# A dependence from a port-sharing VectorE operation to the GpSimd operation planned behind it, in both planned lists of a fused attention and MoE kernel

## The chip, the cores and the metric

The kernel runs on one core of a Trainium2 chip. A core has five instruction queues that run side by side: the profile calls them PE (TensorE, matrix multiplication), DVE (VectorE), ACT (ScalarE), POOL (GpSimd) and SP (SyncE, which here only starts DMA transfers). Each queue runs its instructions in order and waits on semaphores where it needs another queue's result. The metric is the device time of one execution in microseconds. The kernel before took 730.56 us (median of 3 runs, 727.94 to 731.85).

## The reference, cut to what matters

```python
def _attn_ref(x, state):                    # x (8, 8, 512, 64), state (8, 8, 32, 64)
    scale = 1.0 / np.sqrt(D)
    scores = scale * np.matmul(x, state.transpose(0, 1, 3, 2))
    ...                                     # softmax over the 32 states
    xread = np.matmul(a, state)
    scores2 = scale * np.matmul(state, x.transpose(0, 1, 3, 2))
    ...                                     # softmax over the 512 tokens
    sread = np.matmul(a2, x)
    return np.concatenate([xread, sread], axis=2)

def _moe_ref(x, w_in, w_out):               # x (4352, 512), w_in (512, 2048), w_out (2048, 512)
    h = x @ w_in
    g = h * np.cos(h)
    return g @ w_out
```

The attention output, with its heads laid side by side, is the x of the second part. Everything is float32.

## The kernel before, in words

The kernel walks over the 8 batches, two at a time (a pair), and at the end over the 256 rows of read states. For a batch it computes both softmaxes from the same scores, never forms xread, but multiplies the states with w_in first and the attention weights with that product. So a tile of h (128 of the 2048 columns, 512 tokens) is one or two PE products of `aT_all` (attention weights) with `sw_all` (states times w_in). ACT and DVE make g = h cos(h) of it, in the four steps `gate`, `gate2`, `gate3`, `gate4` (a rounding, a difference, a sine table, a product), and g lands in a quarter of `g_all`. From the second pair on the products with both weight matrices use a seven-product scheme instead of eight. The scheme needs sums and differences of its operands, and these sums are the work of POOL: `Product.sums` (halves of g, tile `g_all`), `sw_sums` (tiles `sw_all` and `swS_all`, needed by the next h tile) and `Product.total` (tile `held`, an output sum). Some sums are on DVE: `outer_sum` (tile `g_all`, 128x1024) and `halves` (tile `aS_all`).

The softmax of the next batch runs in the shadow of the tiles. Its places that matter here are: `spread1` (L357) writes a broadcast sum into the first half of the tile `xT`; `norm1` (L425) multiplies the attention weights by it on DVE (`aT_all<-aT_all,xT`, 128x1024, two inputs in SBUF); `turn_kept` (L438) then copies the turned second softmax on ACT into the same half of `xT`, so that this copy has to wait for norm1; and `reads` (L445) multiplies with the copy on PE (`at<-x_b,xT`).

The order on every queue is decided when the program is built, by two list planners with a cost for each operation. The first pair of batches is a list of tasks: `first_pair` (L1598) takes the tasks by due time and calls each one, which issues its instructions (the profile puts them all at L44, the line of the helper `Lane`). Everything after it is recorded on a tape, cut into works by `works_of` (L1776), ordered by `in_order` (L1823) and issued in the order of the planned starts (L1868 to L1870; the profile puts these at L1870). Both planners hold that POOL and certain DVE operations share a port of SBUF and don't run at once: in the first list those whose task is added with `shares`, in the second `tensor_tensor` and `scalar_tensor_tensor` works with no operand in PSUM (L1807). `lock` is the planned end of the last operation that used the port, and a sharing operation is planned no earlier (L1651, L1848, L1857). The plan fixes only the order within each queue. Between queues the built program waits for data alone.

POOL issues no DMA after the first four state loads. SP issues all the others in order, among them the weight blocks that PE reads (`g_all<-blocks_kept`) and the x loads into `xT`.

Of the kernel before, what the change touches and what calls it, by code (L numbers as in the profile page):

```python
# [22 lines left out]
def kernel(  # L23
# [8 lines left out]
    tape, taping, burst, exps_bursts = [], [False], [0], set()  # L32
    hbm_names = [a.name for a in (x, state, moe_w_in, moe_w_out, out)]

    class Lane:
        def __init__(self, name, engine):
            self.name, self.engine = name, engine

        def __getattr__(self, op):
            f = getattr(self.engine, op)  # L40

            def call(*args, **kw):
                if not taping[0]:
                    return f(*args, **kw)  # L44
                tape.append((self.name, op, f, args, kw, burst[0]))
            return call

    class Lanes:
        tensor, vector = Lane("pe", tc.nc.tensor), Lane("dve", tc.nc.vector)
# [941 lines left out]
    def warm(n, to):  # L991

        for _ in range(n):
            nc.tensor.matmul(out=to, lhsT=zeros[:, 0:P], rhs=zeros, start=True,
                             stop=True)
# [95 lines left out]
    dve, pool = nc.vector, nc.gpsimd  # L1091
    for n in range(B // 2):
        end = n == B // 2 - 1
# [468 lines left out]
    def link(tasks):  # L1562
        wrote, read = {}, defaultdict(list)
        for t in tasks:
            before = set()
            for r in t.reads:
                before.add(wrote.get(r))
            for w in t.writes:
                before.add(wrote.get(w))
                before.update(read[w])  # L1570
            before.discard(None)
            before.discard(t)
            t.before = list(before)
            for r in t.reads:
                read[r].append(t)
            for w in t.writes:
                wrote[w] = t
                read[w] = []
        after = defaultdict(list)
        for t in tasks:  # L1580
            for u in t.before:
                after[u].append(t)
        for t in reversed(tasks):
            t.due = 22.0 + PACE * t.due if t.due is not None else 1e9
            for u in after[t]:
                t.due = min(t.due, u.due - t.cost - 0.05)
        return after
# [10 lines left out]
    def first_pair():  # L1598
        nonlocal n_stages
        now[0] = FIRST - 1  # L1600
        tasks = first_pair_tasks()
        after = link(tasks)
        free = {"pe": START_PE, "act": 10.2, "dve": 12.8, "pool": 6.0,
                "sp": 23.0}
        arrived = {}
        for i, at_ in enumerate(ARRIVED):
            for r in ("".join(names_raw(i))).split():
                arrived[r] = at_
        waiting = {t: len(t.before) for t in tasks}
        ready = {t: 0.0 for t in tasks}  # L1610
        for t in tasks:
            for r in t.reads:
                if r in arrived:
                    ready[t] = max(ready[t], arrived[r])
            for w in t.writes:
                arrived.pop(w, None)
        can = [t for t in tasks if not waiting[t]]
        lanes = 22.0
        lock = 0.0
        cold = True  # L1620
        log = []
        while can:
            best = None
            for e in free:
                mine = [t for t in can if t.engine == e]
                if not mine:
                    continue
                starts = {}
                for t in mine:
                    asked = max(free[e], ready[t])  # L1630
                    shares = t.shares or e == "pool"
                    starts[t] = max(asked, lock) if shares else asked
                soon = min(starts.values())
                t = min((t for t in mine if starts[t] <= soon + NEAR),
                        key=lambda t: t.due + 8.0 * (starts[t] - soon))
                asked = max(free[e], ready[t])
                if best is None or (starts[t], asked) < best[0:2]:
                    best = starts[t], asked, t
            at_, _, t = best
            if t.engine == "pe":  # L1640
                idle = int((at_ - free["pe"] - .4) / .86)
                if t.writes[0] == "acc":
                    cold = False
                if cold and idle > 0:
                    warm(idle, acc[0])
            t.what()
            can.remove(t)
            end = at_ + t.cost
            free[t.engine] = end
            log.append((at_, t))  # L1650
            if t.shares or t.engine == "pool":  # L1651
                lock = end
            if t.engine == "sp":
                size = {"x": .13, "Q": 1.05, "B": .26, "r": .26}.get(
                    t.writes[0][0], .3)
                lanes = max(lanes, at_ + 1.3) + size / .36
                end = lanes - 1.8
            t.end = end
            for u in after[t]:
                waiting[u] -= 1  # L1660
                ready[u] = max(ready[u], end + lag(t, u))
                if not waiting[u]:
                    can.append(u)
        assert len(log) == len(tasks)
        n_stages = 5
        for at_ in [stage_at, sums_at, outer_at]:
            for step in [step for step in at_ if step < FIRST]:
                del at_[step]
        return log

    def names_raw(i):
        h = i % 2
        n = (2 * h, 2 * h + 1) if i < 4 else range(QT)
        return " ".join(f"Q{SLOTS[i]}_{k}" for k in n)
# [101 lines left out]
    def works_of(tape):  # L1776
        works, last, at_ = [], {}, 0.0
        wrote, read = {}, defaultdict(list)
        for engine, op, f, args, kw, n in tape:
            aps = [a for a in list(args) + list(kw.values())  # L1780
                   if isinstance(a, AP)]
            outs = [kw["out"] if "out" in kw else args[0]]
            if "accum_out" in kw:
                outs.append(kw["accum_out"])
            ins = [a for a in aps if not any(a is o for o in outs)]
            if op == "matmul" and not kw["start"]:
                ins.append(outs[0])
            exp = engine == "act" and kw.get("func") == ACTF.Exp
            w = last.get(engine)
            if not (w is not None and w.burst == n  # L1790
                    and (engine == "act" and n in exps_bursts
                         or engine == "pe" and works[-1] is w)):
                w = last[engine] = Work(engine, n, at_)
                works.append(w)
                if exp:
                    w.cost += 2.5
                if op == "matmul" and kw["lhsT"].partition_size() == D:
                    w.cost += .3
            w.calls.append((f, args, kw))
            w.cost += cost_of(engine, op, kw, aps)  # L1800
            if engine == "pe":
                at_ += cost_of(engine, op, kw, aps)
            if op == "dma_start":
                w.landing = landing(kw)
            if engine == "dve" and op in ("tensor_tensor",
                                          "scalar_tensor_tensor"):
                w.shares = all(a.space != PSUM for a in aps)  # L1807
            for cell in [c for a in ins for c in cells(a)]:
                if cell in wrote:
                    w.before.add(wrote[cell])  # L1810
                read[cell].append(w)
            for cell in [c for o in outs for c in cells(o)]:
                if cell in wrote:
                    w.before.add(wrote[cell])
                w.before.update(read[cell])
                wrote[cell] = w
                read[cell] = []
            w.before.discard(w)
        return works
# [3 lines left out]
    def in_order(tape, free):  # L1823
# [15 lines left out]
        while can:  # L1839
            best = None  # L1840
            for e in free:
# [4 lines left out]
                for w in mine:  # L1846
# [3 lines left out]
                w = min((w for w in mine if starts[w] <= soon + NEAR_LATER),  # L1850
                        key=lambda w: w.due + LATE * (starts[w] - soon))
                if best is None or starts[w] < best.start:
                    best, best.start = w, starts[w]
            w = best
            can.remove(w)
            end = free[w.engine] = w.start + w.cost
# [3 lines left out]
            for u in after[w]:  # L1860
# [4 lines left out]
                if not waiting[u]:  # L1865
                    can.append(u)
        assert len(log) == len(works)
        for w in sorted(log, key=lambda w: w.start):  # L1868
            for f, args, kw in w.calls:
                f(*args, **kw)  # L1870

    first_log = first_pair()
    singles.__exit__(None, None, None)
# [72 lines left out]
```

## Time and profile before

| | |
|---|---|
| device time, 3 runs | 727.94, 730.56, 731.85 us |
| device time of the profiled execution | 726.99 us |
| its span, first to last instruction | 725.2 us |
| PE busy | 701.0 us, 97% of the span |
| DVE, ACT, POOL busy | 508.9 (70%), 348.0 (48%), 540.2 (74%) us |
| mean granted TensorE clock | 0.992 |

A profile row of a group names the line, the engine, the operation, the tile it writes and the tiles it reads, the shape, how many there are, and after the bar the busy time and the mean duration of one. In a timeline the row begins with the start and the duration in us from the start of the span. In the view of waits a row says which engine waited for which producer, how long in total, how often, and the longest. In the view by stretches there follow, after the stretch and its length, the busy times of PE, PEld (weight loads), DVE, ACT and POOL with the number of instructions, then the granted TensorE clock as a share of the full one, the busy share of the DMA engines and their rate. What the duration of one DVE or POOL instruction shows includes time in which the port kept it out.

### The profile page before, as it was taken

How to read it: one execution, taken by the hardware profiler on the slowest of the kernel's cores; microseconds unless marked ns; L12 is line 12 of the kernel's file. 1: busy time of each engine (PE TensorE's matmuls, PEld its weight loads, DVE VectorE, ACT ScalarE, POOL GpSimd, SP SyncE). 2: the span in 40 equal slices, each digit the busy share in tenths (PEclk: the TensorE clock that was granted, in tenths of full speed). 3: DMA queues.
4: the chain of work that ended last, by engine and by line, in shares of the span. 5: the costliest groups of instructions: out<-in, count | busy, mean ns of one | idle time of the engine just before them, and what ended most of it. 6: DMA issues, size and time to landing. Idle time of an engine off the chain costs nothing.

```text
span 725.2 us, 10728 instructions
## 1 busy us (share of the span) xinstructions
PE 701.0 (97%) x3628; PEld 524.1 (72%) x3628; DVE 508.9 (70%) x698; ACT 348.0 (48%) x591; POOL 540.2 (74%) x524
## 2 busy tenths in 40 slices
PE   8898899999979999999999999999999999999997
PEld 4444344477857878787788787878788888888886
DVE  4899879987876687776986567878766476625630
ACT  5689876754543447444634554445634443211100
POOL 1466799578984998898998856998988848896500
PEclk9999999999989999999999999999999999999999
DMA  9966699756436754783258435762366345465851
GB/s 298 294 194 201 190 260 294 190 137 142 142 82 134 205 130 123 149 193 89 78 128 186 118 88 126 153 147 85 114 153 157 89 111 128 110 200 170 224 103 29
DMA packets 204022, 111.34 MB, mean 154 GB/s; under 512 B 149888, under 2 KB 166784, under 8 KB 203968
## 3 DMA queue, kind: packets, MB, share of 16 engines
q1 hardware_dynamic: 202880, 110.14, 58.5%
q8 instruction: 29, 0.48, 0.3%
q10 hardware_dynamic: 960, 0.39, 0.2%
q14 instruction: 25, 0.20, 0.1%
q0 software_dynamic: 128, 0.13, 0.1%
HBM read 87.03 MB, written 23.59 MB: 153 GB/s over the span
## 4 chain that ended last, share of the span: by engine, by line
PE 67%; DVE 3%; issue 1%; ACT 1%; DVEq 0%
PE o L1870 38%; PE h L1870 21%; PE at L1870 8%; DVE g_all L1870 1%; ACT q_all L1870 1%; DVE q_all L1870 0%; DVE h L1870 0%; DVE xT L1870 0%; DVE aS_all L1870 0%; ACT L1870 0%; DVE aT_all L1870 0%; DVE held L1870 0%; DVE sr L1870 0%; DVE m_all L1870 0%; ACT xT L1870 0%
## 5 line engine op out<-in xcount | busy, mean ns | idle before, releaser
L1870 POOL TENSOR_TENSOR g_all<-g_all 128x512 f32<-128x512 f32 x250 | 329.2, 1344 | 29.2 <-PE o L1870 20.0
L1870 PE MATMUL o<-g_all 128*128 128x256 f32 x1448 | 341.3, 381 | 0.0
L1870 PEld LDWEIGHTS o<-g_all 128*128 128x128 f32 x1448 | 273.5, 191 | 46.8 <-issue 5.6
L1870 ACT ACTIVATE q_all<-h 128x1024 int32<-128x1024 f32 (+1 forms) x56 | 54.1, 965 | 108.3 <-PE h L1870 106.8
L1870 DVE TENSOR_TENSOR q_all<-q_all,h 128x1024 f32<-128x1024 int32 (+1 forms) x56 | 64.0, 1142 | 53.4 <-ACT q_all L1870 53.3
L1870 DVE TENSOR_TENSOR g_all<-h,q_all 128x1024 f32<-128x1024 f32 (+1 forms) x56 | 64.1, 1145 | 28.0 <-ACT q_all L1870 25.6
L1870 ACT ACTIVATE q_all<-q_all,halfpi 128x1024 f32<-128x1024 f32 (+1 forms) x56 | 61.1, 1091 | 26.1 <-DVE q_all L1870 25.8
L44 PE MATMUL h<-aT_all,sw_all 128*128 128x512 f32 (+1 forms) x132 | 62.8, 603 | 5.4 <-DVE g_all L44 5.4
L1870 DVE TENSOR_TENSOR g_all<-g_all 128x1024 f32<-128x1024 f32 (+1 forms) x68 | 67.8, 1039 | 0.1
L1870 DVE TENSOR_TENSOR h<-h,sums_all 128x256 f32<-128x256 f32 x94 | 40.1, 427 | 38.1 <-PE h L1870 33.2
L1870 PE MATMUL h<-aS_all,swS_all 128*128 128x256 f32 x188 | 59.0, 396 | 0.0
L1870 PE MATMUL h<-aS_all,sw_all 128*128 128x256 f32 x188 | 56.3, 381 | 2.7 <-DVE h L1870 2.7
L1870 POOL TENSOR_TENSOR swS_all<-sw_all 128x128 f32<-128x128 f32 x46 | 22.3, 486 | 47.6 <-ACT sw_all L1870 47.3
L1870 PE MATMUL h<-aT_all,sw_all 128*128 128x256 f32 x188 | 56.6, 383 | 0.0
L44 PEld LDWEIGHTS h<-aT_all,sw_all 128*128 128x128 f32 x132 | 23.9, 192 | 36.0 <-issue 21.5
L1870 PEld LDWEIGHTS h<-aS_all,swS_all 128*128 128x128 f32 x188 | 33.9, 191 | 21.3 <-POOL g_all L1870 9.2
L44 POOL TENSOR_TENSOR g_all<-g_all 128x512 f32<-128x512 f32 x30 | 42.2, 1426 | 5.1 <-DVE g_all L44 2.4
L44 PE MATMUL o<-g_all 128*128 128x512 f32 (+1 forms) x112 | 43.7, 520 | 0.0
L44 POOL TENSOR_TENSOR w_in<-w_in,aS_all 128x1024 int32<-128x1024 int32 (+1 forms) x10 | 21.4, 2153 | 29.5 <-DVE w_in L44 22.3
L1870 PEld LDWEIGHTS h<-aS_all,sw_all 128*128 128x128 f32 x188 | 35.2, 190 | 9.0 <-DVE h L1870 3.4
L1870 PEld LDWEIGHTS h<-aT_all,sw_all 128*128 128x128 f32 x188 | 35.8, 192 | 5.5 <-DVE g_all L1870 0.6
L1870 DVE SCALAR_TENSOR_TENSOR held<-o,held 128x512 f32<-128x512 f32 x38 | 26.1, 687 | 12.9 <-PE o L1870 12.3
(159 smaller groups left out, 960.2 us busy)
## 6 DMA issues: line engine op xcount, KB each, us to landing
g_all<-blocks_kept SPq DMA_DIRECT2D x206, 256.0 KB, 2.8
blocks_kept<-g_all SPq DMA_DIRECT2D x48, 256.0 KB, 4.1
g_all<-in_moe_w_out_dram SPq DMA_DIRECT2D x8, 1024.0 KB, 5.5
out_dram<-ot SPq DMA_DIRECT2D x128, 64.0 KB, 2.8
g_all<-in_moe_w_in_dram SPq DMA_DIRECT2D x6, 1024.0 KB, 7.2
x_b<-in_x_dram SPq DMA_DIRECT2D x24, 256.0 KB, 4.6
xT<-in_x_dram SPq DMA_DIRECT2D x80, 64.0 KB, 2.8
x_b<-in_x_dram SPq DMA_DIRECT2D x16, 128.0 KB, 4.1
```

What stands on the lines that cost most here:

```text
L44: return f(*args, **kw)
L1870: f(*args, **kw)
```

## The change

Each queue's helper now remembers the instruction that it issued last. Both planners remember the planned end of the last DVE operation that shares the port (`dve_end`). When the next POOL operation is issued and its planned start is less than 1.0 us behind that end, it is given a wait for `dve.last`, the instruction that DVE issued last. After any POOL operation `dve_end` is forgotten. The tape carries the helper instead of its name, so that the second list can do the same.

```diff
     class Lane:
         def __init__(self, name, engine):
             self.name, self.engine = name, engine
+            self.last = self.behind = None
...
+        def issue(self, f, args, kw):
+            made = self.last = f(*args, **kw)
+            if self.behind is not None:
+                tc.add_manual_dep(made.ins, self.behind.ins.name,
+                                  mybir.DependencyInfo(
+                                      mybir.DependencyClass.Sync,
+                                      mybir.DependencyReason.DATA),
+                                  reason="ports")
+                self.behind = None
...
+            if t.engine == "pool" and dve_end is not None:
+                if at_ < dve_end + 1.0:
+                    pool.behind = dve.last
+                dve_end = None
             t.what()
             can.remove(t)
             end = at_ + t.cost
+            if t.engine == "dve" and t.shares:
+                dve_end = end
...
+        dve_end = None
         for w in sorted(log, key=lambda w: w.start):
-            for f, args, kw in w.calls:
-                f(*args, **kw)
+            if w.engine == "pool" and dve_end is not None:
+                if w.start < dve_end + 1.0:
+                    pool.behind = dve.last
+                dve_end = None
+            for lane, f, args, kw in w.calls:
+                lane.issue(f, args, kw)
+            if w.engine == "dve" and w.shares:
+                dve_end = w.start + w.cost
```

## The prediction

> **What bounds the kernel now.** First the page's busy times, then the view of waits for PE and for its weight loads (waiter, producer, total, times, longest).
>
> ```profile
> PE 701.0 (97%) x3628; PEld 524.1 (72%) x3628; DVE 508.9 (70%) x698; ACT 348.0 (48%) x591; POOL 540.2 (74%) x524
> ...
> PE at L1870 <- ACT xT L1870: 4.4, 1, 4.4
> PE h L1870 <- DVE h L1870: 2.7, 4, 0.9
> ...
> PEld h L1870 <- POOL g_all L1870: 9.2, 11, 0.8
> ```
>
> PE sets the end: 24 us of the span are not busy, about 19 of them real stalls, 12 before 142 us and 7 after. No PE row names POOL: POOL is last only for weight loads, 0.8 us at most. A later POOL costs time only where it uses up the room before PE reads. Gains can come only from the stalls, so the largest, 4.4 us, is followed back in the timeline (start, duration).
>
> ```profile
> 205.21 7.12 DVE L1870 TENSOR_TENSOR aT_all<-aT_all,xT 128x1024 f32<-128x1024 f32 x1
> 212.25 0.68 DVE L1870 SCALAR_TENSOR_TENSOR held<-o,held 128x512 f32<-128x512 f32 x1
> ...
> 205.09 0.46 POOL L1870 TENSOR_TENSOR swS_all<-sw_all,swS_all 128x128 f32<-128x128 f32 x1
> 205.50 2.48 POOL L1870 TENSOR_TENSOR g_all<-g_all 128x512 f32<-128x512 f32 x2
> 207.94 0.45 POOL L1870 TENSOR_TENSOR swS_all<-sw_all 128x128 f32<-128x128 f32 x1
> 208.35 2.48 POOL L1870 TENSOR_TENSOR g_all<-g_all 128x512 f32<-128x512 f32 x2
> 210.79 0.45 POOL L1870 TENSOR_TENSOR swS_all<-swS_all,sw_all 128x128 f32<-128x128 f32 x1
> 213.01 1.38 POOL L1870 TENSOR_TENSOR held<-held 128x512 f32<-128x512 f32 x1 [1.76 <-DVE held L1870]
> ...
> 212.41 0.58 ACT L1870 COPY xT<-at 128x512 f32<-128x512 f32 x1 [8.77 <-issue]
> ```
>
> The first row is norm1. Unhindered a 128x1024 operation with both inputs in SBUF takes 1.22 us (the quarter point of its kind); this one took 7.12. 212.33 less 1.22 is 211.11, where POOL's run of seven ends (211.24), at an operation that waits for DVE. Norm1 was kept out for 5.9 us. The ACT copy into the same half of `xT` follows its end at 212.41, and PE, free at 208.65, starts its reads at 213.04. What follows stands in the view by stretches (busy PE, PEld, DVE, ACT, POOL, then the granted clock):
>
> ```profile
> 208.70:213.04 4.34, 0.00 (x0) 0.00 (x0) 4.34 (x3) 0.63 (x2) 2.58 (x4) 0.91 0.25 60
> 213.04:216.50 3.46, 3.46 (x20) 2.86 (x21) 2.04 (x3) 2.62 (x5) 2.17 (x3) 0.50 0.10 17
> ```
>
> After the idle stretch PE works at half clock, until 219.06 by the clock records. So the stall costs more than itself.
>
> **The change, part by part.** In the listings of both built programs every queue has the same instructions in the same order; only waits of POOL differ. 71 POOL instructions wait for a later DVE instruction than before, 30 in the first list, 41 in the second. At least 20 name one that doesn't share the port (a transpose, a reciprocal, an operand in PSUM), since `dve.last` is whatever DVE issued last. Behind each waiting instruction stand POOL's later sums; PE waits for the `sw_all`, `swS_all` and `g_all` ones, SP for those it stores, DVE for `held`.
>
> *Norm1 at 205.21.* The POOL sum at 203.03 gets a wait for the DVE operation at 212.25, which stands behind norm1. POOL then idles at 205.21: norm1 ends at 205.21 + 1.22 = 206.43. The next DVE operation has its input since 204.48 and takes 0.68: done at 207.03. The shortest distance from a DVE end to a waiting POOL start in the trace is 0.08, so POOL resumes at 207.11. The ACT copy runs from 206.5 to 207.1, before PE is free at 208.65: the stall of 4.40 goes. The work that ran at half clock, 16 matmuls of reads, 4 of h, 8 of o, took from 213.04 to 219.66, 6.62 us. The same sequence at full clock:
>
> ```profile
> 292.22 1.09 PE L1870 MATMUL at<-x_b,xT 128*64 128x128 f32 x16
> ...
> 294.21 1.89 PE L1870 MATMUL o<-g_all 128*128 128x256 f32 x8
> 295.94 0.38 PE L1870 MATMUL h<-aS_all,sw_all 128*128 128x256 f32 x1
> ```
>
> 295.94 - 292.22 = 3.72, so 2.90 more. Together -7.3. Late next is POOL: the `swS_all` sum behind the waiting one ends near 209.1, and PE wants it at 214.95 - 4.3 = 210.7, so 1.6 is left. POOL stops again at 213.01, for DVE's transpose at 226.07. That one follows PE's reads and becomes about 220.4; the `sw_all` sums behind it end near 222.6, and PE reads them at 231.02, which becomes 226.1. Nothing is lost.
>
> *The stall at 231.02 (0.5).* It ends a DVE chain that starts with two `halves`:
>
> ```profile
> 222.98 1.42 DVE L1870 TENSOR_TENSOR aS_all<-aT_all,aS_all 128x256 f32<-128x256 f32 x1
> 224.32 1.49 DVE L1870 TENSOR_TENSOR aS_all<-aT_all 128x256 f32<-128x256 f32 x1
> 225.74 0.41 DVE L1870 TENSOR_TENSOR aS_all<-aT_all,aS_all 128x256 f32<-128x256 f32 x1
> ```
>
> The third shows the unhindered 0.41; the others each waited for a POOL sum. These sums now come behind the POOL operation held for the transpose, so 2 us of DVE delay go, more than the stall: -0.5.
>
> *The stalls at 355.90 and 509.36 (0.61 each beyond the normal spacing of PE).* The same pattern, once for each pair:
>
> ```profile
> 353.37 2.13 DVE L1870 TENSOR_TENSOR g_all<-g_all 128x1024 f32<-128x1024 f32 x1
> 355.43 0.42 DVE L1870 TENSOR_TENSOR h<-h,sums_all 128x256 f32<-128x256 f32 x1
> ```
>
> A POOL sum that started at 353.14 kept the first out for 0.91. It now waits for the second row, which moves to 354.5; PE gets it at 355.0, before its natural 355.08. Two times: -1.2. The POOL sum starts 1.9 us later; no PE row waits on it soon.
>
> *First list, 30 waits.* Mostly POOL already queued behind a running DVE operation: DVE 17.78 to 18.46, POOL from 18.02 for 1.58 instead of 1.28. A wait makes it start at 18.54 and end 0.22 later. The worst is the `w_in` sum at 19.56: it waits for the reciprocal, ends 0.8 later, and PE has 0.49 of room; but PE then stands until 24.31 for an ACT copy behind a conversion, so nothing comes of it. ACT conversions that follow POOL at once (69.55, 83.55) pass 0.2 on to PE stalls that DVE ends. Bounds: -0.8 if the small DVE stalls between 129 and 140 us shrink, +2 if each conversion passes its delay on. I take +0.3, by the 0.2 rows.
>
> *The other waits of the second list.* They hold POOL for 1 to 5 us in this trace's times; idle gaps of POOL absorb that later (47.3 us of waiting for ACT's `sw_all` copies). The tightest rooms: 1.9 us at 157.92 against a lag of about 1.6, and 4.1 at 482.88 against 2.5 (estimates from these rows, with DVE unhindered). A held-back POOL also meets `halves` that were free (142.90, 309.16): up to 1.1 for DVE, against 0.8 to 1.0 of room before PE. Bounds 0 to +1.5; +0.3, as at most two exceed it. SP stores shift by 1 to 2 us; SP issues the weight blocks 9 to 10 us before PE reads them, and they land 2.8 us after the issue.
>
> **A rule against the change.** The Trainium skill, SBUF — State Buffer, section Who interferes with whom, says that of a DVE instruction with two SBUF inputs and a GpSimd one that reads SBUF, the one that issues first holds the port for its whole instruction and the other is fully blocked until then. By that, the port already orders them: norm1 would have waited 0.34 us, for the POOL operation of 205.09, and the copy would have beaten PE. The change would then only add 71 waits: 0.6 us slower (both allowances). The row says 5.9 us, seven POOL operations in turn; elsewhere (353.37) DVE did get in after one. I take the row; the rule stays as the reason why such runs are rare.
>
> **Sum.** -7.3 - 0.5 - 1.2 + 0.3 + 0.3 = -8.4. The profiled execution, 726.99 with its span of 725.2, becomes 718.6. It is 3.6 below the median of the runs; the same gain from 730.56 gives **722.2 us**.
>
> **Rivals.**
> *Only moved (0.17):* DVE gets in, but the gain is spent again: norm1 is freed, the copy, or another wait on the same PE reads, is late anyway, or a clock drop falls elsewhere. For: PE is the end of every chain and 97% busy. Against: after the copy the rows show no second condition for the reads. 727 to 731; worked at -1.5, the stalls of 0.6 alone with the allowances: 729.1.
> *Backlog, slower (0.15):* POOL held back runs its backlog without a pause, and a later norm1 arriving in it is kept out as the one at 205.21 was, 7.3 us each with the clock. There are such operations at 287.10, 363.15, 440.62 and 518.56. For: POOL is busy 24.62 of 25 us around 350, so nothing absorbs a lag there. Against: the POOL operation just ahead of 363.15 and of 518.56 itself now waits for that norm1, and before 287.10 and 440.62 POOL starts from a pause. It decides from two on: +14.6 - 8.4 = +6.2, 736.8.
> *The dependence doesn't bite:* excluded for the place at 203.03 by the listing, where the wait stands.
>
> **How the numbers follow.** Forecast 0.68, moved 0.17, backlog 0.15. A change under 0.5% (3.65 us) can't be told from none here, so these are also the chances of faster, same and slower. The forecast alone spans 717 to 725: both ends of the allowances and the 2 us by which runs differ. The range for 8 in 10 adds the moved case: 717 to 731.
>
> **What would show it.** Norm1 near 205 at 1.2 to 1.5 us; no PE stall near 209 and no half clock after it; DVE `g_all<-g_all` near 353 and 507 at 1.2; POOL idle near 203 to 207 with a DVE `held` releaser. Wrong: any DVE row over 3 us elsewhere, a PE row waiting for POOL of over 1 us, or the clock halved at a new place.

## The result, and the profile after

The changed kernel takes 720.36 us (median of 4 runs, 717.76 to 722.87) beside 731.13 us (727.94 to 731.85) for the kernel before: ratio 0.9862, 95% interval 0.9823 to 0.9902. In a second comparison on another chip it was 719.5 beside 728.91, ratio 0.9878 (0.9848 to 0.9908). The forecast was 722.2, in a range of 717 to 731. Here and below medians are of all executions, ratios and intervals of the fast ones alone.

The profiled execution of after took 722.87 us, the slowest of its four, and its span is 721.1. Its busy times stand in part 1 of the page, and the view of waits for PE begins as below (waiter, producer, total, times, longest):

```profile
PE 701.0 (97%) x3628; PEld 522.6 (72%) x3628; DVE 484.6 (67%) x698; ACT 348.6 (48%) x591; POOL 508.5 (71%) x524
```

```profile
PE h L51 <- DVE g_all L51: 5.5, 6, 1.9
PE at L51 <- ACT xT L51: 5.0, 4, 2.3
...
PE h L51 <- POOL swS_all L51: 0.2, 1, 0.2
```

All instructions now carry L51, the line of the new `issue`. DVE is 24.3 us less busy than before and POOL 31.7, though both do the same work; this is read as time in which one kept the other out of the port. PE's busy time is what it was, 701.0. The longest wait of PE is now 2.3 us; the one of 4.4 is gone, and by this view POOL is the last producer of a single wait of 0.2.

The place of norm1 in the timeline of after (start, duration), first DVE and POOL, then ACT and PE:

```profile
209.77 1.21 DVE L51 TENSOR_TENSOR aT_all<-aT_all,xT 128x1024 f32<-128x1024 f32 x1
210.91 0.68 DVE L51 SCALAR_TENSOR_TENSOR held<-o,held 128x512 f32<-128x512 f32 x1
...
208.33 1.27 POOL L51 TENSOR_TENSOR g_all<-g_all 128x512 f32<-128x512 f32 x1
211.67 1.38 POOL L51 TENSOR_TENSOR g_all<-g_all 128x512 f32<-128x512 f32 x1 [2.07 <-DVE held L51]
...
211.06 0.59 ACT L51 COPY xT<-at 128x512 f32<-128x512 f32 x1 [2.87 <-PE h L51]
...
211.32 1.89 PE L51 MATMUL o<-g_all 128*128 128x256 f32 x8
213.14 1.09 PE L51 MATMUL at<-x_b,xT 128*64 128x128 f32 x16
```

POOL stands idle for 2.07 us until the `held` operation behind norm1 has ended. Norm1 takes 1.21 us in place of 7.12, the copy is done at 211.65, and PE goes from the product to its reads at 213.14 without a gap.

Since every queue has the same instructions in the same order in both programs, the start of each PE instruction of after can be compared with that of the same one before. The lateness of after, and what each stage adds to it:

| up to | before, us | after, us | lateness | added there |
|---|---|---|---|---|
| end of the first list | 144.34 | 148.90 | +4.56 | +4.56 |
| end of the work behind norm1 | 219.22 | 216.42 | -2.80 | -7.36 |
| the stall at 231 | 231.02 | 227.50 | -3.52 | -0.72 |
| the stall at 356 | 355.90 | 351.49 | -4.42 | -0.90 |
| its next h tile | 363.70 | 359.79 | -3.91 | +0.51 |
| the stall at 509, its next h tile | 517.15 | 513.02 | -4.14 | -0.23 |

The last instruction is 4.06 us earlier. So in these two executions less than half of the gain of the medians is seen: 4.6 us went in the first list. There the after trace shows three stretches of half clock and the before trace one; the two at 70.21 and 94.11 us are new, which the prediction had named as a sign of being wrong. Was that the price of the first list's waits? The experiments answer that.

### The profile page after: what moved, and what is told of

The parts are those of the page before. It is cut to its first block, busy times and chain, and to the rows that moved or that the text cites. A ratio compares the mean times of both kernels' runs of the same rounds, so it can differ in the third digit from the quotient of the medians.

```text
span 721.1 us, 10739 instructions
## 1 busy us (share of the span) xinstructions
PE 701.0 (97%) x3628; PEld 522.6 (72%) x3628; DVE 484.6 (67%) x698; ACT 348.6 (48%) x591; POOL 508.5 (71%) x524
## 4 chain that ended last, share of the span: by engine, by line
PE 67%; DVE 1%; POOL 1%; ACT 1%; issue 0%; DVEq 0%; ACTq 0%
PE o L51 38%; PE h L51 21%; PE at L51 8%; POOL g_all L51 1%; DVE g_all L51 1%; ACT q_all L51 0%; DVE h L51 0%; ACT L51 0%; DVE q_all L51 0%; DVE xT L51 0%; ACT sw_all L51 0%; POOL swS_all L51 0%; DVE held L51 0%; DVE aT_all L51 0%; DVE m_all L51 0%
## 5 line engine op out<-in xcount | busy, mean ns | idle before, releaser
L51 POOL TENSOR_TENSOR g_all<-g_all 128x512 f32<-128x512 f32 x280 | 350.9, 1282 | 49.1 <-DVE g_all L51 24.0
L51 PE MATMUL o<-g_all 128*128 128x256 f32 (+1 forms) x1560 | 384.2, 391 | 0.0
L51 PEld LDWEIGHTS o<-g_all 128*128 128x128 f32 x1560 | 293.6, 190 | 64.8 <-issue 22.7
L51 ACT ACTIVATE q_all<-h 128x1024 int32<-128x1024 f32 (+1 forms) x88 | 73.1, 830 | 124.9 <-PE h L51 123.2
L51 DVE TENSOR_TENSOR q_all<-q_all,h 128x1024 f32<-128x1024 int32 (+1 forms) x88 | 85.5, 973 | 70.8 <-ACT q_all L51 70.8
L51 PE MATMUL h<-aT_all,sw_all 128*128 128x256 f32 (+1 forms) x320 | 122.8, 486 | 5.6 <-DVE g_all L51 5.5
L51 DVE TENSOR_TENSOR g_all<-h,q_all 128x1024 f32<-128x1024 f32 (+1 forms) x88 | 85.8, 977 | 40.4 <-ACT q_all L51 38.8
L51 ACT ACTIVATE q_all<-q_all,halfpi 128x1024 f32<-128x1024 f32 (+1 forms) x88 | 84.0, 957 | 35.7 <-DVE q_all L51 35.2
L51 PEld LDWEIGHTS h<-aT_all,sw_all 128*128 128x128 f32 x320 | 60.6, 194 | 42.9 <-issue 22.2
L51 DVE TENSOR_TENSOR g_all<-g_all 128x1024 f32<-128x1024 f32 (+1 forms) x78 | 72.5, 970 | 0.1
L51 DVE TENSOR_TENSOR h<-h,sums_all 128x256 f32<-128x256 f32 x96 | 41.1, 428 | 37.9 <-PE h L51 33.0
L51 PE MATMUL h<-aS_all,swS_all 128*128 128x256 f32 x192 | 59.7, 393 | 0.0
L51 PE MATMUL h<-aS_all,sw_all 128*128 128x256 f32 x192 | 57.5, 381 | 1.2 <-DVE h L51 1.0
L51 POOL TENSOR_TENSOR swS_all<-sw_all 128x128 f32<-128x128 f32 x48 | 22.0, 457 | 44.6 <-ACT sw_all L51 25.1
L51 PEld LDWEIGHTS h<-aS_all,swS_all 128*128 128x128 f32 x192 | 34.4, 189 | 21.3 <-POOL g_all L51 7.5
L51 POOL TENSOR_TENSOR w_in<-w_in,aS_all 128x1024 int32<-128x1024 int32 (+1 forms) x10 | 19.5, 1959 | 32.8 <-ACT w_in L51 14.7
L51 PEld LDWEIGHTS h<-aS_all,sw_all 128*128 128x128 f32 x192 | 35.9, 190 | 8.0 <-DVE h L51 1.6
L51 DVE SCALAR_TENSOR_TENSOR held<-o,held 128x512 f32<-128x512 f32 x38 | 26.1, 687 | 14.9 <-PE o L51 14.3
L51 ACT COPY sw_all<-at 128x512 f32<-128x512 f32 x48 | 25.8, 591 | 18.4 <-PE at L51 18.0
L51 ACT COPY o<-o 128x256 f32<-128x256 f32 x26 | 9.3, 359 | 46.7 <-PE o L51 46.6
L51 POOL TENSOR_TENSOR g_all<-g_all,aS_all 128x1024 int32<-128x1024 int32 x8 | 18.8, 2359 | 18.0 <-DVE q_all L51 7.4
L51 ACT COPY o<-sums_all 128x256 f32<-128x256 f32 x26 | 9.8, 376 | 44.9 <-PE o L51 44.9
```

Of the source, the lines that this page charges most:

```text
L51: made = self.last = f(*args, **kw)
```

## The experiments

All kernels have the same instructions in the same order as both kernels of the change; only waits of POOL differ. `pool.count` is a counter added to the helper, the number of POOL instructions issued so far; a condition on it picks one operation.

**Which waits bring the gain: one, the second list, the first list, all but norm1's.**

```diff
e1_one_wait, e2_second_list (first list)
-                if at_ < dve_end + 1.0:
+                if False:
e1_one_wait (second list)
-                if w.start < dve_end + 1.0:
+                if pool.count == 108:
e3_first_list (second list)
-                if w.start < dve_end + 1.0:
+                if False:
e4_all_but_two (second list)
-                if w.start < dve_end + 1.0:
+                if w.start < dve_end + 1.0 and pool.count not in (108, 109):
```

> Only one of the 71 waits is left: the POOL sum ahead of norm1 (203.03 in the trace of before) waits for the DVE held operation behind norm1. Theory A (one starved operation): norm1 takes 1.2 to 1.5 us in place of 7.1, the PE stall of 4.4 us and the half clock behind it are gone, and the time falls by 7.3 us, ratio 0.990. The other blocked DVE operations stay, so the stall at 231 (0.5) and the two of 0.6 at 355 and 509 stay. Rival B (many small gains): one wait brings 2 us at most, ratio 0.997 or more, the rest of the gain needs the other 70.

> Only the 41 waits of the second list. Theory A: all gains are in the second list (-7.3, -0.5, -1.2, +0.3), and the first list's waits only cost: in the profile of after, PE is 4.9 us late when the first list ends, some 1.5 of it by later operations and 3.4 by two more stretches at half clock. So this kernel is 1.5 to 3 us faster than after: 717.5 to 719, ratio 0.981 to 0.984. Rival C: the half clock falls where it does by chance, and the first list's waits are neutral: 720.4, ratio 0.986. Rival B: the first list brings a part of the gain: 722 or more.

> Only the 30 waits of the first list. Theory A: norm1 near 208 still takes about 7 us and PE stalls 4.4 us behind it; the first list costs 1.5 us by its waits, or up to 5 with the half clock: ratio 1.002 to 1.007. Rival C: neutral, 1.000. Rival B: ratio below 0.998.

> All waits except the two that hold POOL back for norm1 (the sums at 203.03 and 204.26 in the trace of before). Theory A: norm1 takes about 7 us again, PE stalls over 4 us behind it and the clock is halved after that; what stays is -1.7 from the small stalls and the first list's cost: ratio 0.997 to 1.003. Rival B: the other 69 waits keep most of the gain, ratio 0.992 or less. If norm1 is short here without its wait, it was the timing of POOL, not the wait, that freed it.

| kernel | waits | median, us (before 727.07) | ratio | 95% interval |
|---|---|---|---|---|
| e1_one_wait | 1 | 719.76 | 0.9896 | 0.9854 to 0.9939 |
| e2_second_list | 41 | 720.05 | 0.9892 | 0.9846 to 0.9937 |
| e3_first_list | 30 | 727.41 | 1.0018 | 0.9979 to 1.0058 |
| e4_all_but_two | 69 | 729.12 | 1.0016 | 0.9984 to 1.0047 |

By the medians one wait of 71 brings the whole gain and the 69 others none. The starts of PE tell it more finely. From the end of the first list to the last PE instruction e1 gains 7.7 us; e2 and after gain 8.64 and 8.62, so the 40 other waits of the second list are worth 0.9 us. The timeline of e1 has norm1 free:

```profile
205.60 1.22 DVE L52 TENSOR_TENSOR aT_all<-aT_all,xT 128x1024 f32<-128x1024 f32 x1
```

In e4 norm1 is kept out even longer than before, by ten POOL operations in a row, since the other waits hold POOL back (the sum at 203.03 of before starts at 204.44) and more of the run is still ahead. That costs 1.80 us against before, and the other waits of the second list bring back 1.27, so e4's ratio near 1 is the sum of a loss and a gain. The timeline of e4 for DVE, and its view by stretches (busy PE, PEld, DVE, ACT, POOL, granted clock, DMA share, rate):

```profile
204.68 9.04 DVE L52 TENSOR_TENSOR aT_all<-aT_all,xT 128x1024 f32<-128x1024 f32 x1
```

```profile
208.60:214.40 5.80, 0.00 (x0) 0.00 (x0) 5.80 (x3) 0.60 (x2) 4.04 (x5) 0.91 0.18 45
214.40:221.00 6.60, 6.56 (x29) 5.42 (x30) 3.63 (x5) 3.19 (x5) 0.00 (x0) 0.56 0.25 42
```

PE stands for all of the 5.8 us, then works at about half clock. That is the stall of before, made longer. Rival B (most of the gain from many small ones) has fallen. Theory A had expected e2 to beat after by 1.5 to 3 us; that can't be seen: 0.9892 lies inside the interval of after. (The 4.9 us of its expectation is 4.56 at the PE instruction of the table above.)

**Was norm1 kept out by POOL's run? A wait in its middle.** The run of seven is cut behind its fourth operation (the sum at 208.35 is the fifth of the seven; the expectation calls it the fourth, but its times are those of 208.35).

```diff
e5_mid_run (its only wait; norm1_op is the instruction of norm1)
+            if w.engine == "pool" and pool.count == 115:
+                pool.behind = norm1_op
             for lane, f, args, kw in w.calls:
```

> One wait, in the middle of the run of seven POOL operations that kept norm1 out: the fourth of them (the g_all sum at 208.35 in the trace of before) waits for norm1, the three ahead of it don't. Theory A (norm1 is kept out by POOL's run for as long as that has a next operation): norm1 takes 208.39 + 1.22 - 205.21 = 4.4 us in place of 7.1, the PE stall behind it is 4.4 - 2.7 = 1.7 us, with no half clock or one stretch of it: 3 to 6 us faster, ratio 0.992 to 0.996. Rival D (norm1 waited for something else that came at 211): norm1 stays at 7.1, POOL stands from 208.4 to 212.4, ratio 1.000 or more.

Timeline of e5, DVE, POOL and PE:

```profile
204.61 4.30 DVE L53 TENSOR_TENSOR aT_all<-aT_all,xT 128x1024 f32<-128x1024 f32 x1
...
207.37 0.46 POOL L53 TENSOR_TENSOR swS_all<-sw_all 128x128 f32<-128x128 f32 x1
208.99 2.68 POOL L53 TENSOR_TENSOR g_all<-g_all 128x512 f32<-128x512 f32 x2 [1.16 <-DVE aT_all L53]
...
209.63 1.09 PE L53 MATMUL at<-x_b,xT 128*64 128x128 f32 x16 [1.58 <-ACT xT L53]
```

4.30 us where 4.4 were expected, and a PE stall of 1.58 where 1.7 were. Norm1's own 1.2 us begin where POOL's fourth operation ends, near 207.8. Its time is the length of the run ahead of the wait. The ratio is 0.9924 (0.9898 to 0.9950). Rival D (norm1 waited for something else) has fallen.

**Why only there?** In the trace of before 43 other DVE operations of the form TENSOR_TENSOR from 108 us on took over 0.25 us more than the shortest tenth of their shape, and all but one got in at the end of the POOL operation that was running (363.15, which had asked 0.07 us before an end, got in one later). So POOL doesn't win always. What is special before 205 is that POOL had run since 188.23 without a gap, and that no DVE operation sharing the port had come in between; the longest such run ahead of the 43 others is 10.1 us. Five kernels add one pause of POOL in that stretch, by a wait that names no norm1 and is over when norm1 asks.

```diff
e7_pause (107; e8_short_pause 105, e9_early_pause 100, e10_run_13 96, e11_run_14 95)
+            if w.engine == "pool" and pool.count == 107:
+                pool.behind = dve.last
             for lane, f, args, kw in w.calls:
```

> One wait that doesn't name norm1: the POOL sum at 201.80 in the trace of before, two ahead of the seven, waits for the DVE product g_all that ends at 204.96. POOL so pauses for 3 us just before norm1 asks, and then has ten operations ready behind the one that runs. Theory E (norm1 is kept out because POOL had held the port without a pause since 188): norm1 gets in after one operation and takes 2.4 us, the PE stall goes, ratio 0.990 to 0.992. Theory F (what counts is that POOL has a next operation ready): norm1 is kept out until the run ends near 214.5, takes 10 us, the PE stall grows to 7.5 us: ratio 1.003 to 1.006.

> How short and how far back may the pause be? One wait, of the POOL sum at 200.15 in the trace of before, for the DVE transpose that ends at 200.48: POOL pauses for 0.4 us, and then runs without a break for 4.6 us (six operations) until norm1 asks, with as many ready behind. Theory E (what keeps norm1 out is a long hold without a pause): norm1 gets in after one operation, takes 1.5 to 2.5 us, ratio 0.990. Theory F2 (the pause must fall just before the request; that of 3.2 us at 204 did): norm1 takes about 7 us, ratio 1.000.

> The same pause further back: the POOL sum at 194.00 in the trace of before waits for the DVE sum that ends at 194.72, a pause of 0.8 us, then 10.4 us of POOL without a break until norm1 asks. Elsewhere in the trace of before (353.37, 506.83) a DVE operation got in after 10.1 us of unbroken POOL. Theory E with a limit above 10 us: norm1 short, ratio 0.990. A limit below 10 us, or theory F2: norm1 about 7 us, ratio 1.000.

> The limit of the unbroken hold, by two pauses further back. Here the POOL sum at 190.70 in the trace of before waits for the DVE reduction that ends at 192.01: then POOL runs 13.1 us without a break until norm1 asks. Known so far: let in after one operation at 10.4 us and less, kept out at 16 to 17 us. Theory E gives no number between: if norm1 is short (1.4 to 2.5 us) the limit lies above 13.1, if it takes 7 us, below.

> The same one operation earlier: the POOL sum at 189.46 waits for the DVE sum that ends at 190.82, a run of 14.3 us ahead of norm1. If norm1 is short here too, either the limit lies between 14.3 and 16 us, or it isn't the length of the run but the shift of POOL by each pause that frees norm1.

| kernel | unbroken POOL ahead of norm1's request | norm1, us | time, us (before beside it) | ratio, 95% interval |
|---|---|---|---|---|
| e7_pause | 0.2 us | 2.18 | 720.18 (728.91) | 0.9882, 0.9839 to 0.9925 |
| e8_short_pause | 4.7 us | 1.40 | 724.68 (730.43) | 0.9923, 0.9871 to 0.9974 |
| e9_early_pause | 10.4 us | 1.41 | 721.96 (730.43) | 0.9904, 0.9862 to 0.9946 |
| e10_run_13 | 13.1 us, 12 operations and a part | 1.56 | 719.90 (729.83), one execution each | |
| e11_run_14 | 14.3 us, 13 operations and a part | 8.54 | 726.64 (729.83), one execution each | |
| before, e3, e4, e5 | 16.2 to 17.0 us | 4.30 to 9.04 | above | |

The last two of the five are the sharpest pair. Norm1 asks in both during the same POOL operation, 0.80 and 0.74 us after its start, with the same queue behind it. The timelines of e10, POOL and DVE, and of e11:

```profile
191.92 2.51 POOL L52 TENSOR_TENSOR g_all<-g_all 128x512 f32<-128x512 f32 x2 [1.35 <-DVE m_all L52]
...
205.47 1.45 POOL L52 TENSOR_TENSOR swS_all<-swS_all,sw_all 128x128 f32<-128x128 f32 x1
...
205.04 1.56 DVE L52 TENSOR_TENSOR aT_all<-aT_all,xT 128x1024 f32<-128x1024 f32 x1
```

```profile
189.11 3.73 POOL L52 TENSOR_TENSOR g_all<-g_all 128x512 f32<-128x512 f32 x3 [1.40 <-DVE h L52]
...
203.89 0.44 POOL L52 TENSOR_TENSOR swS_all<-swS_all,sw_all 128x128 f32<-128x128 f32 x1
...
203.41 8.54 DVE L52 TENSOR_TENSOR aT_all<-aT_all,xT 128x1024 f32<-128x1024 f32 x1
```

In e10 the next POOL operation grows from 0.44 to 1.45 us: it is POOL that stands while norm1 runs. In e11 it keeps its 0.44, as do all that follow, and norm1 waits for the whole run. Theories F and F2 (a queue of ready operations, or a pause that must fall just before) have fallen: a pause of 0.33 us, 4.7 us ahead, with the queue behind it full, is enough. e11 also pauses and shifts POOL, by 1.4 us, and norm1 is shut out all the same, so a shift of POOL isn't what frees it; and what DVE had done before is the same in all five. Between 13.1 and 14.3 us something turns, by one execution of each kernel. Whether it counts time or operations isn't settled (both grew together), nor which mechanism does it.

**The named operation, and the change once more.**

```diff
 # e6_named: second list only
                 if w.start < dve_end + 1.0:
-                    pool.behind = dve.last
+                    pool.behind = shared
...
             if w.engine == "dve" and w.shares:
                 dve_end = w.start + w.cost
+                shared = dve.last
```

> Second list only, and the wait names the last DVE operation that shares the port in place of whatever DVE issued last. Theory A: POOL waits less, no PE row depends on it: equal to the second list alone within 0.5 us, ratio 0.989, and 1 us below after. Rival B: the waits for operations that don't share the port cost something, 1 to 2 us less than the second list alone.

> The changed kernel once more, beside the others on one chip. Theory A: 0.986 to 0.991; in the trace PE is 1.1 us later than before at the end of the first list where both have as many stretches at half clock, and each further stretch there costs 1.5 to 1.7 us; the time differs from run to run by the number of these stretches, 0 to 3. Rival C (the waits of the first list make the clock drop): three stretches again.

718.69 us, ratio 0.9869 (0.9839 to 0.9899), beside 719.50 and 0.9878 (0.9848 to 0.9908) for the change itself on the same chip, with 728.91 before. The clean comparison for the name is e2, which has the same list with `dve.last`: by the starts of PE its second list gains 8.64 us and that of e6 8.63. So waiting for operations that don't share the port costs nothing there, and no version tried beats the change beyond the intervals. The repeated change has one stretch of half clock in the first list and not three, and PE is 1.20 us late there beside the 1.1 expected.

## Why the prediction was right

**Norm1 (forecast -7.3): right, and to the tenth.** In all nine traces in which norm1 was free (1.2 to 2.2 us), PE gains 7.36 us on the trace of before between the products ahead of the reads and the work behind them: 4.47 by the start of the reads and 2.89 behind it, where before ran at half clock. The tenth is owed to comparing with the very execution that the forecast was read from. In e3 norm1 takes 7.09 us and the stall is the same, but one stretch of half clock follows it and not two, and 1.25 us less was lost. The step that took the row against the rule of the Trainium skill (SBUF — State Buffer, Who interferes with whom: the first to issue holds the port for its whole instruction, and the other waits until then) decided the forecast, and e5 and e11 bear it out: the rule tells what happened at 42 of the 44 places counted above, but at norm1's it would have had DVE in after 0.34 us, and the change 0.6 us slower. The checks of what comes next were less exact: they moved PE's later reads by the stalls and not by the half clock. The `swS_all` sum was to have 1.6 us of room and has 0.7 in after (its end at 213.47, PE's read at 214.16), and 231.02 less 7.3 is 223.7, not 226.1. Nothing came of it.

**The stall at 231 (forecast -0.5): -0.72.** Right in kind: in after the three `halves` are unhindered.

```profile
220.17 0.42 DVE L51 TENSOR_TENSOR aS_all<-aT_all,aS_all 128x256 f32<-128x256 f32 x1
220.51 0.42 DVE L51 TENSOR_TENSOR aS_all<-aT_all 128x256 f32<-128x256 f32 x1
220.85 0.42 DVE L51 TENSOR_TENSOR aS_all<-aT_all,aS_all 128x256 f32<-128x256 f32 x1
```

But e1, without the wait for the transpose that the forecast gave as the reason, gains 0.61 of it, with halves of 1.37, 0.67 and 0.68 us; its expectation had this stall stay. So most of it needs no more than norm1's own wait.

**The stalls at 356 and 509 (forecast -1.2 together): -0.62.** The stalls went as forecast, 0.90 and 0.64, but 0.51 and 0.41 came back in the next h tile. The forecast named no second limit there; it is ACT, whose queue runs without a gap into the cosine that this tile needs. ACT and DVE in after:

```profile
354.31 1.08 ACT L51 COPY sw_all<-at 128x512 f32<-128x512 f32 x2
355.26 0.27 ACT L51 ACTIVATE i_all<-i_all 128x34 f32<-128x34 f32 x1
355.54 1.28 ACT L51 ACT_TABLE_LOAD   x1
356.83 1.15 ACT L51 ACTIVATE q_all<-q_all,halfpi 128x1024 f32<-128x1024 f32 x1
...
358.08 1.23 DVE L51 TENSOR_TENSOR g_all<-h,q_all 128x1024 f32<-128x1024 f32 x1 [0.52 <-POOL swS_all L51]
359.23 0.42 DVE L51 TENSOR_TENSOR h<-h,sums_all 128x256 f32<-128x256 f32 x1
```

The DVE product starts 0.10 us behind the cosine's end at 357.98 (in the program it waits for ACT; the POOL operation that the view names only ended nearby), and the sum behind it lets PE start at 359.79. In before ACT had the same sequence 3.60 us later, while PE was 4.42 later: before, the sum had ended 0.45 ahead of PE's start, 0.30 more than the 0.15 it needs now, so 0.82 - 0.30 = 0.52 comes back.

**The other waits of the second list (forecast +0.3): +0.08.** That is what is left in after when the three places above are taken from the 8.62 us that its second list gains.

**The first list (forecast +0.3, bounds -0.8 to +2): not resolved, and it hides the size of the gain.** What the end of the first list owes to the clock is seen in kernels without any wait there. Lateness of the PE instruction at 144.34, by the number of half-clock stretches ahead of it:

| stretches | no waits in the first list | with its 30 waits |
|---|---|---|
| 0 | -1.80 (e11) | -0.83 (e3), -0.53 (e4) |
| 1 | 0 (before), +0.02 (e2), +0.13 (e8), -0.17 (e10), +0.38 (e1), -0.60 (e5) | +1.20 (after_again) |
| 2 | +1.98 (e7), +2.76 (e6) | |
| 3 | +4.42 (e9) | +4.56 (after) |

So a stretch goes with some 2 us, and nearly all of the 4.56 of the after trace are two more stretches, which e9 had as well without one of these waits. By the rows of the table the waits cost from 0.1 us (three stretches) to 1.3 (none; against the lowest of the middle row 1.8); e3's interval (-0.2 to +0.6%) can't say more. That the stretches fall by chance (rival C of e2) stands; that the first list's waits cause them (what the expectation of the repeated change calls rival C) has fallen, since e3, e4 and that repetition have these waits and none, none and one.

**The sum.** For the second list the forecast had -8.7, and all four kernels with its waits (after, its repetition, e2, e6) gain 8.62 to 8.64. That this agrees to a tenth is luck in part: 0.6 too much for the small stalls at 356 and 509 is made up by 0.2 too little at 231 and 0.2 too much cost for the other waits. With as many stretches on both sides, -8.62 and the first list's 0.1 to 1.3 make -7.3 to -8.5; the forecast had -8.4. The medians differ by 10.8 and, in the second comparison, 9.4, where the interval is 6.7 to 11.1 us. The profiled 726.99 that the sum was made against had one early stretch; runs of before with a granted clock of 0.987 took 729.8 to 734.6, those with 0.994 or 0.995 took 725.0 to 726.8. For after, 1.000 goes with 717.76 and 0.993 with 722.87.

**The rivals.** *Only moved* happened for 0.9 of the 1.5 us of the small stalls and for nothing of norm1. *Backlog* did not happen: the norm1 operations at 283.50 and 514.50 in after took 1.48 and 1.85 us, each behind one POOL operation, and no DVE operation was kept out by more than 2.1. What the rival lacked was the condition found above, a long unbroken hold. POOL runs of 14 to 19 us remain in after (from 261.1, 628.1, 591.0); none of DVE's `g_all`, `aS_all` or `aT_all` sums on SBUF operands came in them, so they don't test the condition.

## What to carry to other kernels

A duration far above its kind was worth more here than the many small ones: one DVE operation of 7.12 us in place of 1.22 held 1% of this kernel, and one dependence out of 71 returned it. Where DVE and GpSimd share work from SBUF, look for GpSimd queues that run long without a pause, and give them one wait ahead of the DVE operation that others need; here each of the four pauses tried within 13.1 us of the request did. Before a few us in the early part of a kernel are put down to an edit, count the half-clock stretches in both traces, and compare PE's starts instruction by instruction.

## What the runs showed of the hardware that was not expected

*The port.* Let in after one POOL operation in 13.1 us and less of unbroken POOL, shut out to the end of the run, or to a wait in it, at 14.3 us and more: so in every kernel run, but at this one place. Whether it holds elsewhere isn't shown.

*The clock.* Half clock comes in stretches of 3.413 us on a grid that lies differently in each run. The same PE stall ahead of 69 us (2.07 us beyond the normal spacing, in both traces) halved the clock in after and not in before. The view by stretches, cut on each trace's own grid, of before and then of after:

```profile
65.46:68.87 3.41, 1.76 (x11) 0.99 (x9) 2.42 (x5) 3.38 (x4) 3.41 (x2) 1.00 0.97 331
68.87:72.29 3.42, 3.16 (x8) 1.49 (x9) 3.38 (x7) 2.83 (x4) 0.65 (x1) 1.00 0.51 185
```

```profile
66.80:70.21 3.41, 1.50 (x10) 1.09 (x9) 3.00 (x6) 2.91 (x4) 3.41 (x2) 1.00 0.95 327
70.21:73.62 3.41, 3.41 (x5) 1.33 (x4) 3.31 (x6) 2.42 (x3) 0.96 (x1) 0.50 0.53 191
```

PE was busy for 1.76 of 3.41 us (0.51) in before's stretch and for 1.50 (0.44) in after's; the next one ran at 1.00 and at 0.50. In the 14 traces all 15 full-clock stretches (up to 250 us) with PE busy for 0.41 or less were followed by half clock, 6 of 11 with 0.43 to 0.46, and none above. The Trainium skill (TensorE: Matmul & The Clock Gate, What's actually happening) has the window of 3413 ns and that it runs freely; that a window needn't be idle, only under 0.41 to 0.46 busy, is what these traces add. So the time of one and the same kernel moves by about 2 us for a stall of about 2 us, by where the grid happens to lie: after and its repetition, with three stretches and one, were 4.56 and 1.20 us late.
